# A hand-written scheduler with new transfer times: output projection two blocks late, q weights in halves, LayerNorm in pairs of tiles

## The chip, the cores and the metric

The kernel runs on one core of a Trainium2 chip. Time is device time in microseconds (us) for one execution. The core has a matrix engine (PE, TensorE; PEld is its weight load), a vector engine (DVE), an engine for activation functions (ACT), a general one (POOL, GpSimd) and one that issues transfers (SP). Each engine executes its own instructions in the order of the program, and they wait for each other through semaphores.

## The reference: what is computed

One layer of attention with 16 query heads that share one key and one value head, then a layer that sends 8 chosen tokens through a gated feed-forward network. x has 2048 tokens of 448 channels; a head has 28.

```
x = A_x
h = x + _A_ref(_layernorm(x))        # q = x wq (16 heads), k = x wk, v = x wv,
                                     # softmax(q k^T / sqrt(28)) v, then wo
h2 = h + _B_ref(_layernorm(h))       # r = x w_r; the 8 tokens with the largest r:
                                     # silu(x wg) * (x wu), then wd, times sigmoid(r);
                                     # the other tokens pass unchanged
```

## The kernel before

**Tiles and blocks.** The 2048 tokens are 16 tiles of 128. Attention runs over 16 blocks of queries (one tile each, all heads). A block has 64 score tiles of 128 keys by 512 query columns: 16 key tiles j times 4 groups of heads i, each in one row strip of PE.

**Two ways to the exponential.** ACT does most tiles: PE writes up to three score tiles into three PSUM banks (0 to 2 for even units, 3 to 5 for odd ones), and one ACT instruction (L712, `act_unit`) turns them into P. In blocks 1 to 15, 16 of the 64 tiles go through DVE instead: PE writes one score tile with each unit into bank 6 (VB), DVE rounds it to the bits of a bf16 exponential (Y, L737), and after four such tiles a batch is shifted into three further copies, two by DVE and one by POOL (Y, L746 and L748). The matmuls with V (`act_pv`, `dve_pv`) add P and the four Y copies into bank 7 (ACC). A block of 48 ACT tiles is so cut into 17 units, "slots" 0 to 16, of three tiles each but for three that have two. `TWO` names these three. A two-wide unit has a bank to spare, which can be lent: before, in slot 5 to the q projection of block b+2, in slot 10 to nothing (that slot carries no DVE tile either), in slot 14 to the output projection of block b-1. The borrowed bank has to be copied out by DVE before the unit but one may write it. P has room for 24 tiles and the P·V matmuls are due `LAG` = 4 units behind.

**Closing a block.** When all P·V matmuls of a block are done, DVE copies ACC to Ot (`close_acc`, L757), due 5.2 units into the next block. `post_block` (L592) then sends the softmax denominators through DRAM: Ot to scratch, back in another layout (Lc), a reciprocal on DVE (Rc, L596), to scratch, and back broadcast over partitions (Rb). POOL multiplies Ot by Rb into On, in two halves (L602). `out_proj` (L605) then multiplies On by wo on PE, adds x on DVE (hbuf, L610), takes LayerNorm 2 of the tile (statistics on DVE, a power and two scalings on POOL, L622, L637, L640) and the router's product (junk, r_col, L643 and L646).

**The head.** x, wk, wq and wv are loaded; ACT copies the weights into padded layouts (wk_rep, wq_pad); LayerNorm 1 (`ln1`, L524) runs by groups of tiles: one, one, two, and then four at a time. The first three groups take the root as Ln and Exp on ACT and are normalised on DVE (xn, L541); the others take a power on POOL and are normalised on POOL (L550) with a product nmr from DVE. `kv` (L554) transposes the normalised tiles on PE and makes K and V from them. Key tile j is needed by the units of block 0 in the order of j.

**The tail.** After the last block come the ranking of the router's values, the expert layer for the 8 tokens, and the output.

**Who sets the order.** All instructions are first collected as operations with an engine, a duration in ns, what they read and write, and a due time (`prio`, from `at(...)`, in tiles of ACT's work: a block is 64). `_Graph.plan` (L145) then plays the program through in Python: each engine takes the ready operation with the smallest due time; DVE holds itself back for the operations marked urgent (`dve_choice`); PE has rules of its own for changes of mode, and idle stretches in the plan are filled with multiplications by zero. The order found this way is fixed in the program. A result counts as available when its operation ends plus a latency of the engine; for a transfer that was 2000 ns after the issue, whatever its size and however many were under way. If a transfer takes longer on the chip than in the plan, an instruction that waits for it holds up all that the plan put behind it on its engine.

Of the kernel before, what the change touches and what calls it, by code (L numbers as in the profile page):

```python
# [19 lines left out]
class _Op:  # L20
    __slots__ = ("eng", "fns", "dur", "lat", "deps", "prio", "idx", "dma", "start", "end", "sig", "name",
                 "pred_left", "succs", "ready", "mode", "pos", "hold", "port", "urgent", "blk")


class _Graph:

    LAT = {PE: 217.0, AC: 185.0, DV: 140.0, PO: 190.0, SP: 0.0}
    SWITCH = 95.0
# [16 lines left out]
    def op(self, eng, fns, dur, reads=(), writes=(), prio=None, dma=False, name="", mode=None, pos=(0, 1, 2, 3),  # L45
           hold=None, deps=(), port=False, urgent=False, blk=None):
        o = _Op()
        o.eng, o.dur, o.dma, o.name = eng, float(dur), dma, name
        o.mode, o.pos, o.hold, o.port, o.urgent, o.blk = mode, pos, hold, port, urgent, blk
        o.fns = list(fns) if isinstance(fns, (list, tuple)) else [fns]  # L50
        o.lat = 2000.0 if dma else self.LAT[eng]
# [93 lines left out]
    def plan(self):  # L145
# [15 lines left out]
        self.todo = {}  # L161
# [9 lines left out]
        while left:  # L171
# [142 lines left out]
def _main(nc, G, sb, ps, psb, flag, scr, A_x, A_wq, A_wk, A_wv, A_wo, B_w_r, B_w_gate, B_w_up, B_w_down, out,  # L314
# [22 lines left out]
    nmr = sb("nmr", [128, NT], F32)  # L337
# [96 lines left out]
    def dma(o, i, writes, reads=(), prio=None):  # L434
        return G.op(SP, lambda e: e.dma_start(o, i), 60, reads=reads, writes=writes, dma=True, prio=prio)  # L435

    dma(x_sb[:, 0, :], x_v[:, 0, :], [("x", 0)])
    dma(wk_sb[0:CK, :, :], A_wk.rearrange("(k p) n -> p k n", p=CK), ["wk_sb"])
    dma(wq_sb[0:CK, :, :], A_wq.rearrange("(k p) n -> p k n", p=CK), ["wq_sb"])
    dma(x_sb[:, 1, :], x_v[:, 1, :], [("x", 1)])  # L440
    dma(x_sb[:, 2:4, :], x_v[:, 2:4, :], [("x", t) for t in range(2, 4)])
    dma(wv_sb[0:CK, :, :], A_wv.rearrange("(k p) n -> p k n", p=CK), ["wv_sb"])
    for i in range(4, NT, 4):
        dma(x_sb[:, i:i + 4, :], x_v[:, i:i + 4, :], [("x", t) for t in range(i, i + 4)])
# [29 lines left out]
    for h in range(2):  # L474
        G.op(AC, lambda e, h=h: e.activation(
            wq_pad[0:CK, 2 * h:2 * h + 2, :, :].rearrange("p k g (i c) -> p k (g i) c", c=32)[:, :, :, 0:DH],
            wq_sb[0:CK, 2 * h:2 * h + 2, :].rearrange("p k (h d) -> p k h d", d=DH), ACT.Identity), 950,
            reads=["wq_sb"], writes=["wq_pad"])
# [5 lines left out]
    for i in range(4):  # L484
        dma(wo_pad[32 * i + 1:32 * i + 1 + DH, :, :], wo_v[i], ["wo_pad"])
    dma(w_rb[:, :], B_w_r.partition_broadcast(128), ["w_rb"])
    dma(wg_sb[0:CK, :, :], B_w_gate.rearrange("(k p) n -> p k n", p=CK), ["wg_sb"])
    dma(wu_sb[0:CK, :, :], B_w_up.rearrange("(k p) n -> p k n", p=CK), ["wu_sb"])
    dma(wd_sb[:, :, :], B_w_down.rearrange("(k p) n -> p k n", p=128), ["wd_sb"])
# [32 lines left out]
    GROUPS = [[0], [1], [2, 3], [4, 5, 6, 7], [8, 9, 10, 11], [12, 13, 14, 15]]  # L522

    def ln1(c):  # L524
# [10 lines left out]
        if c < 3:  # L535
# [56 lines left out]
    def post_block(b):  # L592
# [6 lines left out]
        dma(Rb[:, rb, :], scr[b, 1].unsqueeze(1).broadcast_to([4, 32, 512]), [("Rb", rb)], reads=[("scr1", b)])  # L599
# [52 lines left out]
    TWO = (5, 10, 14)  # L652
    LAG = 4
    slots = []
# [11 lines left out]
    for x in vt:  # L666
        if slots[n][0] and slots[n][1] == TWO[1]:
            n += 1
        slots[n][3] = x
        n += 1  # L670
# [133 lines left out]
    else:  # L804
# [22 lines left out]
        for b in range(NB):  # L827
            at(64.0 * b + 64.0 + (LAG + 1.2) * m0, close_acc, b)
            if b:
                if b + 2 < NB:  # L830
                    at(64.0 * b + TWO[0] * m0 + 0.1, lambda b=b: q_project(b + 2, misc(b, TWO[0])))
                at(64.0 * b + TWO[2] * m0 + 0.1, out_proj, b - 1, misc(b, TWO[2]))
        for b in (1, 2):
            at(24.0 + 8 * b, lambda b=b: q_project(b, ring_bank()))
        at(64.0 * NB + (LAG + 1.3) * m0, out_proj, NB - 1, 0)
        for c in range(len(GROUPS)):
            t = 4.0 * GROUPS[c][0]
            at(t - (40.0 if c < 4 else 24.0), ln1, c)
            at(t - (39.9 if c < 4 else 23.9) , kv, c)
# [198 lines left out]
```

## Time and profile before

| | us |
|---|---|
| median of 3 runs | 496.29 |
| lowest and highest | 489.58, 497.11 |
| the profiled execution | 492.97 |
| its span, first to last instruction | 491.2 |
| PE, DVE, ACT, POOL busy in it | 347.6, 339.8, 372.7, 198.7 |
| first exponential of block 0, of block 1 | 15.20, 51.35 |
| last exponential ends | 431.77 |

How to read the rows: "L712" is a line of the kernel. A row of the timeline has the start, the length, the engine, the line, the operation, what it writes and reads, their shapes, how many instructions are merged, and in brackets the idle time of the engine ahead of it and what ended it. A row of waits has the total, the number and the longest. A row of the chain of waits has a start, a length and the name of what the end waited for. In a table of stretches each engine has its busy time and number of instructions, then come the granted clock of PE and the share and rate of the transfers. All matmuls are recorded under L418 and all transfers under L435, so they are told apart by what they write and read; "ps" is any PSUM bank.

### The profile page before, as it was taken

The page shows a single profiled execution, that of the slowest core. Times are in us where ns is not written, and L with a number is a line of the kernel's source. Part 1 is how long each engine was busy: PE and PEld are TensorE (multiplying, and loading weights), DVE is VectorE, ACT ScalarE, POOL GpSimd, SP SyncE. Part 2 cuts the span into 40 slices and gives each one's busy share as a digit, 9 for nine tenths or more (in the row PEclk, how much of TensorE's full clock was granted, in tenths as well). Part 3 has the DMA queues.
Part 4 walks back from the last instruction along what each step waited for, and adds up shares of the span by engine and source line. Part 5 has one row for each costly group of instructions (what it writes and reads, how often), then busy time and mean ns, then how long its engine had stood idle before and what let it go on. Part 6 is the DMA issues. An engine that isn't in the chain of part 4 may idle for free.

```text
span 491.2 us, 8685 instructions
## 1 busy us (share of the span) xinstructions
PE 347.6 (71%) x3571; PEld 118.9 (24%) x3571; DVE 339.8 (69%) x675; ACT 372.7 (76%) x305; POOL 198.7 (40%) x197
## 2 busy tenths in 40 slices
PE   1888777786768777876777776777786777711585
PEld 1443222122221222121212121212122222200540
DVE  6943778586967787687868586959586878634423
ACT  3579899888987989798979688978888899911012
POOL 3670344354544444344444453525444444641000
PEclk9799999889997999799989699989879999965565
DMA  8950000000000000000000000000000000000004
GB/s 226 247 144 7 3 24 3 22 3 24 3 23 1 24 1 25 1 25 1 25 2 21 3 3 23 3 21 3 23 1 24 3 24 3 24 22 3 0 3 155
DMA packets 15958, 14.69 MB, mean 30 GB/s; under 512 B 5976, under 2 KB 12904, under 8 KB 15912
## 3 DMA queue, kind: packets, MB, share of 16 engines
q1 hardware_dynamic: 15912, 14.05, 10.0%
q8 instruction: 31, 0.51, 0.4%
q14 instruction: 15, 0.12, 0.1%
HBM read 11.94 MB, written 2.10 MB: 29 GB/s over the span
## 4 chain that ended last, share of the span: by engine, by line
DVE 36%; PE 24%; DMA 19%; POOL 9%; ACT 6%; issue 3%; SPq 1%; POOLq 0%
PE ps L418 23%; DVE Y L737 16%; DMA Rb<-l_scr 14%; DVE Y L746 8%; ACT P L712 6%; POOL Y L748 5%; DMA l_scr<-Rc 4%; POOL On L602 3%; DVE Q L518 2%; DVE Ot L757 2%; DVE hbuf L610 2%; DVE junk L643 2%; DMA x_sb<-in_A_x_dram 1%; DVE r_col L646 1%; SPq L435 1%
## 5 line engine op out<-in xcount | busy, mean ns | idle before, releaser
L712 ACT ACTIVATE P<-ps 128x1536 bf16<-128x1536 f32 (+2 forms) x281 | 361.4, 1378 | 59.1 <-PE ps L418 57.7
L737 DVE TENSOR_SCALAR Y<-ps 128x512 int16<-128x512 f32 x240 | 164.9, 687 | 93.9 <-PE ps L418 93.1
L748 POOL TENSOR_TENSOR Y<-Y,step 128x1024 int32<-128x1024 int32 x60 | 113.5, 1892 | 147.7 <-DVE Y L746 110.7
L418 PE MATMUL ps<-Q,K 32*128 32x512 bf16 x1024 | 119.3, 401 | 75.7 <-DVE Y L737 49.6
L418 PE MATMUL ps<-Y,Vs 128*32 128x512 bf16 x960 | 93.2, 404 | 21.5 <-POOL Y L748 19.0
L746 DVE TENSOR_SCALAR Y<-Y 128x2048 int16<-128x2048 int16 x120 | 86.9, 735 | 0.1
L418 PE MATMUL ps<-P,Vs 128*32 128x512 bf16 x784 | 77.5, 401 | 0.6 <-ACT P L712 0.6
L418 PEld LDWEIGHTS ps<-Q,K 32*128 32x128 bf16 x1024 | 32.9, 91 | 180.9 <-ACT P L712 116.1
L602 POOL TENSOR_TENSOR On<-Ot,Rb 128x256 bf16<-128x256 f32 x32 | 24.3, 763 | 62.6 <-DMA Rb<-l_scr 62.6
L418 PE MATMUL ps<-zero 128*32 128x512 bf16 x107 | 38.3, 422 | 0.0
L418 PEld LDWEIGHTS ps<-Y,Vs 128*32 128x32 bf16 x960 | 23.6, 95 | 57.9 <-POOL Y L748 23.0
L418 PEld LDWEIGHTS ps<-P,Vs 128*32 128x32 bf16 x784 | 18.8, 94 | 39.6 <-issue 36.7
L418 PE MATMUL ps<-wo_pad,On 128*128 128x448 bf16 x64 | 19.2, 428 | 8.2 <-POOL On L602 8.2
L637 POOL TENSOR_SCALAR x_sb<-hbuf,st 128x448 bf16<-128x448 f32 x15 | 17.6, 1170 | 4.8 <-DVE st L626 4.8
L418 PE MATMUL ps<-xnT,wq_pad 112*128 112x128 bf16 x256 | 18.2, 226 | 0.1
L610 DVE TENSOR_TENSOR hbuf<-ps,x_sb 128x448 f32<-128x448 f32 x16 | 9.8, 616 | 10.0 <-PE ps L418 10.0
L418 PEld LDWEIGHTS ps<-xnT,wq_pad 112*128 112x128 bf16 x256 | 15.1, 101 | 4.0 <-issue 3.6
L940 ACT ACTIVATE xnT<-ps 128x448 bf16<-128x448 f32 x8 | 4.4, 545 | 12.9 <-PE ps L418 12.9
L421 PE MATMUL ps<-ident,xn 128*112 128x128 bf16 x64 | 6.0, 249 | 10.6 <-DVE xn L541 10.6
L418 PEld LDWEIGHTS ps<-zero 128*32 128x32 bf16 x107 | 9.2, 99 | 17.0 <-issue 15.0
L518 DVE TENSOR_SCALAR Q<-ps,qone 128x512 bf16<-128x512 f32 x16 | 11.8, 738 | 2.0 <-PE ps L418 2.0
L622 POOL TENSOR_TENSOR st<-st,nhalf 128x1 f32<-128x1 f32 x15 | 8.3, 552 | 11.0 <-DVE st L614 11.0
(125 smaller groups left out, 204.8 us busy)
## 6 DMA issues: line engine op xcount, KB each, us to landing
Rb<-l_scr SPq DMA_DIRECT2D x16, 256.0 KB
out_dram<-xnT SPq DMA_DIRECT2D x4, 448.0 KB, 3.3
wg_sb<-in_B_w_gate_dram SPq DMA_DIRECT2D x1, 1568.0 KB, 13.5
wu_sb<-in_B_w_up_dram SPq DMA_DIRECT2D x1, 1568.0 KB, 19.7
wd_sb<-in_B_w_down_dram SPq DMA_DIRECT2D x1, 1568.0 KB, 23.3
x_sb<-in_A_x_dram SPq DMA_DIRECT2D x3, 448.0 KB, 6.0
wq_sb<-in_A_wq_dram SPq DMA_DIRECT2D x1, 392.0 KB, 4.1
wo_pad<-in_A_wo_dram SPq DMA_DIRECT2D x4, 98.0 KB
```

What stands on the lines that cost most here:

```text
L418: return lambda e: e.matmul(o, lhsT=l, rhs=r, start=start, stop=stop)
L518: G.op(DV, lambda e: e.tensor_scalar(Q[:, q, :, :].rearrange("p g n -> p (g n)"), ps[:, bank, :], qone[:, 0:1], None, ALU.add), dvt(512), ...
L602: G.op(PO, lambda e, c=c: e.tensor_tensor(On[:, rb, c], Ot[:, rb, c], Rb[:, rb, c], ALU.mult), 750, reads=[("Ot", rb), ("Rb", rb)], writes ...
L610: G.op(DV, lambda e: e.tensor_tensor(hbuf[:, hr, :], ps[:, bank, 0:D], x_sb[:, t, :], ALU.add), dvt(D), reads=[pk(bank), ("x", t)], writes ...
L622: G.op(PO, lambda e: e.tensor_tensor(st[:, t, 4:5], st[:, t, 7:8], nhalf[:, 0:1], ALU.pow), 600, reads=[("st7", t), "nhalf"], writes=[("st ...
L637: G.op(PO, lambda e: e.tensor_scalar(outf[:, t, :], hbuf[:, hr, :], st[:, t, 5:6], st[:, t, 6:7], ALU.mult, ALU.add), 800, reads=[("h", hr ...
L643: G.op(DV, lambda e: e.scalar_tensor_tensor(junk[:, :], hbuf[:, hr, :], st[:, t, 4:5], w_rb[:, :], ALU.mult, ALU.mult, accum_out=st[:, t, ...
L712: G.op(AC, lambda e: e.activation(P[:, s0:s0 + w, :], ps[:, b0:b0 + w, :], ACT.Exp, bias=-(ZERO + SHIFT) * OCT, scale=OCT), w * 427 + 50, ...
L737: G.op(DV, lambda e: e.tensor_scalar(Y[:, y, 0, q, :].bitcast(I16), ps[:, VB, :], 0.0, 32639.0 - STEP[3], ALU.max, ALU.min), dvt(512), rea ...
L746: done = [G.op(DV, lambda e, c=c: e.tensor_single_scalar(y[c].bitcast(I16), y[0].bitcast(I16), STEP[c], ALU.add), 600, reads=r, writes=[(" ...
L748: G.op(PO, lambda e: e.tensor_tensor(y[3].bitcast(I32), y[0].bitcast(I32), step3[:, 0:1].broadcast_to([128, 1024]), ALU.add), 2050, reads= ...
L757: o = G.op(DV, lambda e: e.tensor_copy(Ot[:, b % 2, :], ps[:, ACC, :]), dvt(512), reads=[pk(ACC)], writes=[("Ot", b % 2)], prio=G.prio - 1 ...
```

## The change

The planner gets other times. A transfer is available 2700 ns after its issue instead of 2000, and Rb's 3900. Loads from the inputs carry their size (`kb`): their landing is counted from a running time at which the transfers before them are done, at 0.19 kB per ns. An operation of DVE or ACT that waits for one on the same engine gets its result after 85 or 110 ns instead of 140 or 185. Some of the work is moved or cut otherwise:

- wq is loaded in two halves, each needed by one of the two ACT copies into wq_pad; wv is loaded ahead of x tiles 2 and 3.
- LayerNorm 1 and `kv` run in groups of 1, 1, 2, 2, ... tiles. The first five groups (tiles 0 to 7) use Ln and Exp on ACT, the other four the power on POOL; all tiles are normalised on DVE. nmr and the POOL scaling are gone.
- The slots with two tiles are 2, 5 and 11. The output projection of block b-2 is due in slot 2 of block b, the q projection of b+2 in slot 5, and slot 11 carries no DVE tile. The projection of block 14 comes at the end of the stream in the DVE tiles' bank, that of block 15 after it as before.
- The q projections of blocks 1 and 2, made in block 0, are due at 14 and 34 instead of 32 and 40; groups up to tile 7 are due 40 ahead of their use, the others 24.

```diff
@@ _Graph
+    SELF = {DV: 85.0, AC: 110.0}
...
-        o.lat = 2000.0 if dma else self.LAT[eng]
+        o.lat = 2700.0 if dma else self.LAT[eng]
...
-        self.todo = {}
+        self.todo, self.dma_end = {}, 700.0
...
+                if c.dma and c.kb:
+                    self.dma_end = max(self.dma_end, s + 2100.0) + c.kb / 0.19
+                    c.lat = self.dma_end - c.end
...
-                r = c.end + c.lat if (sem or n.eng != c.eng) else c.start
+                r = c.end + (self.SELF.get(n.eng, c.lat) if n.eng == c.eng else c.lat) if (
+                    sem or n.eng != c.eng) else c.start
@@ _main: loads
-    dma(x_sb[:, 0, :], x_v[:, 0, :], [("x", 0)])
-    dma(wk_sb[0:CK, :, :], A_wk.rearrange("(k p) n -> p k n", p=CK), ["wk_sb"])
-    dma(wq_sb[0:CK, :, :], A_wq.rearrange("(k p) n -> p k n", p=CK), ["wq_sb"])
-    dma(x_sb[:, 1, :], x_v[:, 1, :], [("x", 1)])
-    dma(x_sb[:, 2:4, :], x_v[:, 2:4, :], [("x", t) for t in range(2, 4)])
-    dma(wv_sb[0:CK, :, :], A_wv.rearrange("(k p) n -> p k n", p=CK), ["wv_sb"])
+    load_x(0, 1)
+    dma(wk_sb[0:CK, :, :], A_wk.rearrange("(k p) n -> p k n", p=CK), ["wk_sb"], kb=25)
+    for h in range(2):
+        dma(wq_sb[0:CK, 2 * h:2 * h + 2, :], wq_v[:, 2 * h:2 * h + 2, :], [("wq_sb", h)], kb=196)
+    load_x(1, 2)
+    dma(wv_sb[0:CK, :, :], A_wv.rearrange("(k p) n -> p k n", p=CK), ["wv_sb"], kb=25)
+    load_x(2, 4)
...
-            reads=["wq_sb"], writes=["wq_pad"])
+            reads=[("wq_sb", h)], writes=["wq_pad"])
@@ _main: LayerNorm 1
-    GROUPS = [[0], [1], [2, 3], [4, 5, 6, 7], [8, 9, 10, 11], [12, 13, 14, 15]]
+    GROUPS = [[0], [1], [2, 3], [4, 5], [6, 7], [8, 9], [10, 11], [12, 13], [14, 15]]
...
-        if c < 3:
+        if c < 5:
...
-            G.op(DV, lambda e: e.scalar_tensor_tensor(nmr[:, sl], mv[:, sl, 0], -1.0, rstd[:, sl], ALU.mult, ALU.mult),
-                 80, reads=[("mv", t) for t in tl] + [("rstd", c)], writes=[("nmr", c)])
             for t in tl:
-                G.op(PO, lambda e, t=t: e.tensor_scalar(xn[:, t, :], x_sb[:, t, :], rstd[:, t:t + 1], nmr[:, t:t + 1],
-                                                        ALU.mult, ALU.add), 770,
-                     reads=[("x", t), ("nmr", c), ("rstd", c)], writes=[("xn", t)])
+                G.op(DV, lambda e, t=t: e.tensor_scalar(xn[:, t, :], x_sb[:, t, :], mv[:, t, 0:1], rstd[:, t:t + 1],
+                                                        ALU.subtract, ALU.mult), 300,
+                     reads=[("x", t), ("mv", t), ("rstd", c)], writes=[("xn", t)])
@@ post_block
-        dma(Rb[:, rb, :], scr[b, 1].unsqueeze(1).broadcast_to([4, 32, 512]), [("Rb", rb)], reads=[("scr1", b)])
+        dma(Rb[:, rb, :], scr[b, 1].unsqueeze(1).broadcast_to([4, 32, 512]), [("Rb", rb)], reads=[("scr1", b)]).lat = 3900.0
@@ the stream
-    TWO = (5, 10, 14)
+    TWO = (2, 5, 11)
...
-        if slots[n][0] and slots[n][1] == TWO[1]:
+        if slots[n][0] and slots[n][1] == TWO[2]:
             n += 1
...
-                    at(64.0 * b + TWO[0] * m0 + 0.1, lambda b=b: q_project(b + 2, misc(b, TWO[0])))
-                at(64.0 * b + TWO[2] * m0 + 0.1, out_proj, b - 1, misc(b, TWO[2]))
+                    at(64.0 * b + TWO[1] * m0 + 0.1, lambda b=b: q_project(b + 2, misc(b, TWO[1])))
+                if b > 1:
+                    at(64.0 * b + TWO[0] * m0 + 0.1, out_proj, b - 2, misc(b, TWO[0]))
         for b in (1, 2):
-            at(24.0 + 8 * b, lambda b=b: q_project(b, ring_bank()))
+            at(20.0 * b - 6.0, lambda b=b: q_project(b, ring_bank()))
+        at(64.0 * NB - 0.1, out_proj, NB - 2, VB)
...
-            at(t - (40.0 if c < 4 else 24.0), ln1, c)
-            at(t - (39.9 if c < 4 else 23.9) , kv, c)
+            at(t - (40.0 if c < 5 else 24.0), ln1, c)
+            at(t - (39.9 if c < 5 else 23.9), kv, c)
```

More of the change, by code (lines that the diff above doesn't have):

```diff
@@ L21 @@
     __slots__ = ("eng", "fns", "dur", "lat", "deps", "prio", "idx", "dma", "start", "end", "sig", "name",
-                 "pred_left", "succs", "ready", "mode", "pos", "hold", "port", "urgent", "blk")
+                 "pred_left", "succs", "ready", "mode", "pos", "hold", "port", "urgent", "blk", "kb")
 class _Graph:
     LAT = {PE: 217.0, AC: 185.0, DV: 140.0, PO: 190.0, SP: 0.0}
+    SELF = {DV: 85.0, AC: 110.0}
     SWITCH = 95.0
@@ L432, in _main, with dma, load_x @@
     x_v = A_x[0].rearrange("(n p) d -> p n d", p=128)
-    def dma(o, i, writes, reads=(), prio=None):
-        return G.op(SP, lambda e: e.dma_start(o, i), 60, reads=reads, writes=writes, dma=True, prio=prio)
-    dma(x_sb[:, 0, :], x_v[:, 0, :], [("x", 0)])
-    dma(wk_sb[0:CK, :, :], A_wk.rearrange("(k p) n -> p k n", p=CK), ["wk_sb"])
-    dma(wq_sb[0:CK, :, :], A_wq.rearrange("(k p) n -> p k n", p=CK), ["wq_sb"])
-    dma(x_sb[:, 1, :], x_v[:, 1, :], [("x", 1)])
-    dma(x_sb[:, 2:4, :], x_v[:, 2:4, :], [("x", t) for t in range(2, 4)])
-    dma(wv_sb[0:CK, :, :], A_wv.rearrange("(k p) n -> p k n", p=CK), ["wv_sb"])
+    def dma(o, i, writes, reads=(), prio=None, kb=0):
+        return G.op(SP, lambda e: e.dma_start(o, i), 60, reads=reads, writes=writes, dma=True, prio=prio, kb=kb)
+    def load_x(a, b):
+        dma(x_sb[:, a:b, :], x_v[:, a:b, :], [("x", t) for t in range(a, b)], kb=112 * (b - a))
+    wq_v = A_wq.rearrange("(k p) n -> p k n", p=CK)
+    load_x(0, 1)
[5 more added lines that the diff above has]
+    load_x(2, 4)
     for i in range(4, NT, 4):
-        dma(x_sb[:, i:i + 4, :], x_v[:, i:i + 4, :], [("x", t) for t in range(i, i + 4)])
+        load_x(i, i + 4)
     G.op(PO, lambda e: e.iota(idi[:, :], [[1, 128]], base=0, channel_multiplier=-1), 250, writes=["junk"])
```

15 lines of the change are left out of this document (7 added, 8 removed).

## The prediction

> **What bounds the kernel now.** I read the page first, then the waits, then the chain of waits, and last the timelines of ACT and POOL through one block of attention, because shares over the whole span mix a head, sixteen blocks and a tail.
>
> ```profile
> PE 347.6 (71%) x3571; PEld 118.9 (24%) x3571; DVE 339.8 (69%) x675; ACT 372.7 (76%) x305; POOL 198.7 (40%) x197
> POOL On L602 <- DMA Rb<-l_scr: 62.6, 16, 5.7
> ACT P L712 <- PE ps L418: 57.7, 64, 4.3
> ```
>
> No engine is full. ACT, which does the exponentials, is the fullest, and the time it loses is lost waiting for scores from PE (57.7 us in 64 waits). POOL loses 62.6 us in 16 waits, one a block, for the transfer that broadcasts the softmax denominators (Rb). POOL is only 40% busy, so the question is what stands behind it in its queue.
>
> ```profile
> 189.75 4.64 DMA Rb<-l_scr
> ...
> 208.96 0.60 DVE Ot L757
> ...
> 213.27 0.66 DVE Q L518
> ...
> 216.13 4.85 DMA Rb<-l_scr
> 221.04 0.73 POOL On L602
> 221.77 1.86 POOL Y L748
> 223.68 2.30 PE ps L418 x19
> 226.00 0.69 DVE Y L737
> 226.70 0.54 DVE hbuf L610
> ...
> 235.11 0.60 DVE junk L643 x2
> ...
> 241.02 4.63 DMA Rb<-l_scr
> ```
>
> This is the chain through one block, each line starting where the one above released it. Rb lands 4.85 us after its issue. Only then does POOL multiply (On); only after that does it make the fourth copy of a batch of shifted scores (Y L748), which the P·V matmuls on PE wait for; and the next score matmuls stand behind those in PE's order. The batch had nothing to do with Rb. From Rb to Rb this block took 241.02 - 216.13 = 24.89 us and the one ahead of it 216.13 - 189.75 = 26.38 us.
>
> ```profile
> 86.64 4.98 DMA Rb<-l_scr
> ...
> 397.62 4.62 DMA Rb<-l_scr
> ```
>
> Twelve such periods, blocks 2 to 13, take (397.62 - 86.64) / 12 = 25.92 us each.
>
> ```profile
> 214.51 9.08 ACT L712 ACTIVATE P<-ps 128x1536 bf16<-128x1536 f32 x7 [0.90 <-PE ps L418]
> 224.45 1.02 ACT L712 ACTIVATE P<-ps 128x1024 bf16<-128x1024 f32 x1 [0.85 <-PE ps L418]
> 226.00 1.45 ACT L712 ACTIVATE P<-ps 128x1536 bf16<-128x1536 f32 x1 [0.53 <-PE ps L418]
> 228.00 2.79 ACT L712 ACTIVATE P<-ps 128x1536 bf16<-128x1536 f32 x2 [0.55 <-PE ps L418]
> ```
>
> ACT's own view of that block has four holes. The first, 0.90, comes from the q projection: its bank is copied late, as the chain shows (Q at 213.27, behind a DVE queue). The second, 0.85, is the batch held up by Rb. The third and fourth, 0.53 and 0.55, are the output projection and its copy (hbuf, 226.70). So ACT without holes needs 24.89 - 2.83 = 22.0 us a block; the seven units from 214.51 give 9.08 / 20 = 0.454 us a tile, and 48 tiles make 21.8, which agrees.
>
> **The change, part by part.** *Measured transfer times in the planner.* No instruction is added. The planner believed a transfer lands 2.0 us after issue; with the new 2.7 and, for Rb, 3.9, its sum from the accumulator copy (Ot) to On rises from about 8.7 to 12.7 us (0.14 + three times 2.76 or 2.06, 3.96 or 2.06, and the reciprocal).
>
> ```profile
> 227.90 1.89 POOL L748 TENSOR_TENSOR Y<-Y,step 128x1024 int32<-128x1024 int32 x1 [3.60 <-DVE Y L746]
> ```
>
> On the chip Ot ends at 209.56 and Rb lets On start at 221.04, 11.5 us later. So On will be planned behind the batch of 221.77 and in front of that of 227.90, seen here in POOL's timeline, where Rb has landed and a POOL hole of 3.60 us takes both halves (2 x 0.73). Queued behind On are then only that later batch and the LayerNorm steps of an output projection; none waits for a transfer. The 0.85 goes to zero.
>
> *Output projection two blocks late.* Moved are four matmuls, hbuf, two statistics steps, one power on POOL, two small DVE steps, two POOL scalings, the router product and its sum; no transfer is among them. It passes POOL's next two batches and the whole q projection on PE and DVE, and gets some 4 us between On and its use where it had none (13.8 slots of 1.3 us, less 12.7 and the two halves). Its own price remains: four matmuls, then a bank that DVE must copy before the next unit but one may write it. The nearest rows are in the last block, where On was in time:
>
> ```profile
> 405.79 1.45 ACT L712 ACTIVATE P<-ps 128x1536 bf16<-128x1536 f32 x1 [0.26 <-PE ps L418]
> 407.79 10.67 ACT L712 ACTIVATE P<-ps 128x1536 bf16<-128x1536 f32 x8 [0.55 <-PE ps L418]
> ```
>
> That is 0.26 + 0.55 = 0.81, against 0.53 + 0.55 = 1.08 now; below, 0.5 would remain if hbuf met an empty DVE. I take 0.81. *The q projection* keeps slot 5; whether DVE is free for its copy depends on an order that I can't see, so 0.3 to 0.90, and I take 0.90. Two-wide slots are still three a block, at other places: nothing. A block then takes 22.0 + 0.90 + 0.81 = 23.7 us (22.8 to 24.0), a gain of 2.2 us, and twelve of them 26.6. Blocks 1, 14 and 15 lack one of the two projections and hardly change. The last projection but one now falls after the stream; its steps hide under the last block's own Rb chain, 11.5 us long, in which POOL otherwise idles: nothing, or the 0.81 of one projection if that cover failed.
>
> *The head.* These are rows of DVE and ACT, in the order of time:
>
> ```profile
> 2.88 0.63 DVE L529 BATCH_NORM_STATS2 bn<-x_sb 128x6 f32<-128x448 bf16 x1 [0.28 <-DMA x_sb<-in_A_x_dram]
> ...
> 6.01 0.63 DVE L529 BATCH_NORM_STATS2 bn<-x_sb 128x6 f32<-128x448 bf16 x1 [2.44 <-DMA x_sb<-in_A_x_dram]
> 10.08 0.69 DVE L541 TENSOR_SCALAR xn<-x_sb,mv,rstd 128x448 bf16<-128x448 bf16 x2
> ```
> ```profile
> 5.74 1.93 ACT L475 ACTIVATE wq_pad<-wq_sb 112x896 bf16<-112x896 bf16 x2 [1.82 <-DMA wq_sb<-in_A_wq_dram]
> ...
> 15.20 3.71 ACT L712 ACTIVATE P<-ps 128x1536 bf16<-128x1536 f32 x3 [3.89 <-PE ps L418]
> 20.20 3.28 ACT L712 ACTIVATE P<-ps 128x1024 bf16<-128x1024 f32 x3 [1.29 <-PE ps L418]
> 27.82 6.89 ACT L712 ACTIVATE P<-ps 128x1536 bf16<-128x1536 f32 x6 [4.33 <-PE ps L418]
> ...
> 51.35 1.45 ACT L712 ACTIVATE P<-ps 128x1536 bf16<-128x1536 f32 x1 [0.61 <-PE ps L418]
> ```
>
> Tile 0 has its statistics at 3.51, and then DVE stands 2.44 us in front of tile 1, which the old plan thought there; the normalised tile comes at 10.08. With tile 1 planned behind it, xn can follow at about 5. The next to be late is wq_pad, finished at 7.67 now; in halves, ACT can start on the first about 1 us sooner, so about 6.7. The extra issue on SP delays the later x tiles by half a microsecond, which nothing near them waits for. The first exponentials start at about 10.7 instead of 15.20. From there block 0 can be bound by ACT or by DVE, which loses 0.16 of nmr for each group of four and gains the xn of twelve tiles from POOL.
>
> ```profile
> L529 DVE BATCH_NORM_STATS2 bn<-x_sb 128x6 f32<-128x448 bf16 x16 | 9.5, 607 | 3.5 <-DMA x_sb<-in_A_x_dram 3.5
> L565 DVE COPY xnT<-ps 112x1024 bf16<-112x1024 bf16 x7 | 4.7, 687 | 4.3 <-PE ps L421 4.3
> L531 DVE BATCH_NORM_AGGREGATE mv<-bn 128x2 f32<-128x6 f32 x16 | 2.3, 163 | 0.0
> ...
> L541 DVE TENSOR_SCALAR xn<-x_sb,mv,rstd 128x448 bf16<-128x448 bf16 x4 | 1.4, 384 | 0.0
> ...
> L575 DVE TENSOR_SCALAR K<-ps,kb 128x256 bf16<-128x256 f32 x1 | 0.5, 468 | 0.0
> ...
> L582 DVE TENSOR_TENSOR Vs<-ps,vone 128x64 bf16<-128x64 f32 x1 | 0.2, 215 | 0.0
> L533 DVE TENSOR_SCALAR var<-mv 128x2 f32<-128x2 f32 x1 | 0.2, 160 | 0.0
> ```
>
> A pair costs DVE 2 x (0.607 + 0.163 + 0.384) + 0.687 + 0.468 + 2 x 0.215 + 0.160 = 4.05 us (Vf is priced as Vs); seven pairs from about 8.5, when tile 0's steps are done, end at 37 with the two Q copies still to come. ACT needs 10.7 + 64 x 0.454 = 39.8, and has the Ln and Exp of two more groups. So ACT bounds it by a little, and I allow 2.7 us for those and for holes where there were 1.29 + 4.33: block 1 starts at 42.5 instead of 51.35, a gain of 8.8 (11 with no holes, 4.5 if only the start moves).
>
> *Sum.* 491.2 - 26.6 - 8.8 = 455.8, and 492.97 - 491.2 = 1.8 around the span makes 457.6. The profiled execution lies 0.7% under the median of the runs; I predict 457 for the median.
>
> **A rule against it.** The granted clock:
>
> ```profile
> 193.00:198.00 5.00, 2.71 (x33) 0.81 (x26) 2.08 (x4) 4.36 (x5) 3.26 (x3) 1.00 0.04 14
> 198.00:203.00 5.00, 4.55 (x32) 0.82 (x30) 3.32 (x6) 2.68 (x3) 0.87 (x1) 0.52 0.00 0
> ```
>
> PE was busy 2.71 of 5 us around the hold-up behind Rb, and the granted clock (the column after POOL) then falls to 0.52. That is why blocks of 26.38 and 24.89 alternate, and my 23.7 takes the full clock. The Trainium skill, in TensorE: Matmul & The Clock Gate, section What's actually happening, gives the loss only to a window of about 3.4 us without work. By that rule gaps of this size neither cost the clock nor give it back, and the loss would stay; the rows, with work in every such stretch, speak against it.
>
> **The rivals.** *The clock still falls in every second block.* It costs (26.38 - 24.89) / 2 = 0.75 a block, 9 in all: 466. For it speaks that PE still pauses at both projections, against it that the longest pause is the one removed. *DVE is crowded.* hbuf, statistics, Ot, Q and the router product now fall together in slots 2 to 7. With Ot's 0.60 and Q's 0.66 on the chain, and 0.6 for each of the others, that is 3.0 us; the Y tiles (0.69) leave 0.67 in each unit of 1.36 us (three tiles at 0.454), 4.0 in six slots, of which four batch copies take 2.4. The 1.4 too much would meet a bank that PE waits for: 1.4 x 13 = 18, 475. Against it: statistics and product may slip. *Only the head moves, and little:* the stream takes another wait as long as the one removed, and block 0 is bound by DVE: 492.97 - 4.5 = 488.5. *Slower:* Ot is planned behind the whole chain of the output projection, eight slots long now. P has room for 24 tiles, eight units, and P·V runs about five behind, so from 3.7 us of lateness ACT stops; a chain of 8.4 us (hbuf at 226.70 to junk at 235.11) costs 4.7 a block, 13 x 4.7 = 61: 518. Against it: the planner gives Ot the higher rank.
>
> **How the numbers follow.** Forecast 0.58, clock 0.12, crowded DVE 0.16, head only 0.09, slower 0.05. The forecast's own bounds are 457 - 2.2 - 12 x 0.9 = 444 and 457 + 4.3 + 12 x 0.3 = 465; up to 476 the range takes in the clock and the crowded DVE. Three runs of before lie 1.5% apart, so some 2% can be told from no change: faster 0.86 (the first three), same 0.09, slower 0.05.
>
> **What would show it.** Right: On waits for Rb no longer, or under 5 us before the last block; a period of Rb near 23.7; first exponentials near 10.7 and block 1 near 42.5; granted clock at 1.0 through the stream; ACT holes only at the two projections. Wrong: a POOL hole ended by Rb; Ot later against its block; DVE without holes while ACT has them; a hole of 2 us at Q or hbuf.

## The result and the profile after

| | before | after |
|---|---|---|
| median of 4 runs, us | 492.94 | 457.36 |
| lowest and highest | 488.21, 497.11 | 456.32, 458.43 |
| the profiled execution, its span | 492.97, 491.2 | 457.83, 455.6 |
| first exponential of block 0, of block 1 | 15.20, 51.35 | 11.32, 50.96 |
| last exponential ends | 431.77 | 396.96 |

The ratio of the times is 0.9313 (0.9239 to 0.9387). Ratios here and below leave out runs that had a lower granted clock than the others of their kernel; the profiled run of one experiment, x3, is of that kind. The forecast of 457 was met, but the last two rows of the table already say that it was not met in the way it was made: block 1 starts 0.4 us sooner, not 8.8, and the stretch from there to the last exponential shrank from 380.4 to 346.0 us, by 34.4 and not by 26.6.

The page of after, with the busy times, the granted clock in 40 slices, and the engines' shares of the chain that ended last:

```profile
PE 335.5 (74%) x3583; PEld 121.5 (27%) x3583; DVE 343.5 (75%) x696; ACT 370.3 (81%) x309; POOL 188.6 (41%) x198
PEclk9999999999999999999999999999999999955565
DVE 49%; PE 32%; ACT 10%; issue 5%; POOL 1%; DMA 1%; POOLq 0%; SPq 0%
```

The waits of after (total, number, longest):

```profile
ACT P L719 <- PE ps L422: 26.7, 31, 3.0
POOL On L609 <- DMA Rb<-l_scr: 7.3, 2, 5.3
```

The old wait of 62.6 us in 16 is 7.3 in 2, and one of the two is the last block's own. ACT's wait for scores has halved. The clock's row shows 9 from the first slice to the end of the stream, where before it dipped every third slice or so. Two pieces at half speed hide in it: the head, shown below, and 55.70 to 59.11, where the column reads 0.50. POOL's timeline in one block shows the order that the forecast described:

```profile
207.88 1.41 POOL L609 TENSOR_TENSOR On<-Ot,Rb 128x256 bf16<-128x256 f32 x2
211.77 1.90 POOL L755 TENSOR_TENSOR Y<-Y,step 128x1024 int32<-128x1024 int32 x1 [2.48 <-DVE Y L753]
```

The multiplication On has no idle time in front of it, and the batch behind it waits for its own data. ACT's timeline of this block and the next has one hole a block:

```profile
198.98 18.24 ACT L719 ACTIVATE P<-ps 128x1536 bf16<-128x1536 f32 x14
218.19 7.96 ACT L719 ACTIVATE P<-ps 128x1536 bf16<-128x1536 f32 x6 [0.96 <-PE ps L422]
```

Four holes (0.90, 0.85, 0.53, 0.55) have become one of 0.96. What makes it stands in PE's timeline and then DVE's:

```profile
214.14 0.93 PE L422 MATMUL ps<-wo_pad,On 128*128 128x448 bf16 x4
...
217.74 0.40 PE L422 MATMUL ps<-Q,K 32*128 32x512 bf16 x4 [0.22 <-DVE hbuf L617]
...
219.26 0.40 PE L422 MATMUL ps<-xnT,wq_pad 112*128 112x128 bf16 x4
```
```profile
216.38 0.68 DVE L764 COPY Ot<-ps 128x512 f32<-128x512 f32 x1
216.98 0.61 DVE L617 TENSOR_TENSOR hbuf<-ps,x_sb 128x448 f32<-128x448 f32 x1
...
219.99 0.74 DVE L527 TENSOR_SCALAR Q<-ps,qone 128x512 bf16<-128x512 f32 x1
```

The projection is done at 215.07, but DVE copies Ot first and hbuf, which frees the bank, second, so the score matmuls start only at 217.74. The q projection, done at 219.66, has its copy at 219.99 and costs ACT nothing. Block 0 went otherwise. ACT's timeline:

```profile
11.32 1.45 ACT L719 ACTIVATE P<-ps 128x1536 bf16<-128x1536 f32 x1 [3.02 <-PE ps L422]
...
18.64 3.28 ACT L719 ACTIVATE P<-ps 128x1024 bf16<-128x1024 f32 x3 [1.20 <-PE ps L422]
24.26 2.37 ACT L719 ACTIVATE P<-ps 128x1536 bf16<-128x1536 f32 x2 [2.33 <-PE ps L422]
...
45.66 2.37 ACT L719 ACTIVATE P<-ps 128x1536 bf16<-128x1536 f32 x2 [1.55 <-PE ps L422]
...
50.96 3.71 ACT L719 ACTIVATE P<-ps 128x1536 bf16<-128x1536 f32 x3 [0.61 <-PE ps L422]
```

and PE's, with the stretches 18 to 24 and 24 to 28 us (length, then busy times of PE, PEld, DVE, ACT, POOL):

```profile
7.70 1.86 PE L422 MATMUL ps<-xnT,wq_pad 112*128 112x128 bf16 x16 [0.61 <-DVE mv L540]
...
24.55 1.10 PE L425 MATMUL ps<-ident,xn 128*112 128x128 bf16 x8
...
29.11 0.65 PE L425 MATMUL ps<-ident,xn 128*112 128x128 bf16 x8
```
```profile
18.00:24.00 6.00, 5.54 (x38) 2.43 (x38) 4.85 (x18) 3.28 (x3) 1.97 (x6) 1.00 1.03 218
24.00:28.00 4.00, 4.00 (x27) 1.80 (x23) 2.68 (x8) 3.16 (x3) 1.50 (x5) 1.00 1.07 251
```

The same eight transposes take 1.10 us at 24.55 and 0.65 at 29.11: until about 28.4 PE runs at half speed, and from 18 to 28 it is busy nearly all the time (9.54 of 10 us) while ACT waits. The clock's column says 1.00 here only because this trace has no clock record before that point; the lengths of the matmuls tell.

### The profile page after: what moved, and what is told of

Read it like the earlier page. It is cut to its first block, busy times and chain, and to the rows that moved or that the text cites. A ratio compares the mean times of both kernels' runs of the same rounds, so it can differ in the third digit from the quotient of the medians.

```text
span 455.6 us, 8732 instructions
## 1 busy us (share of the span) xinstructions
PE 335.5 (74%) x3583; PEld 121.5 (27%) x3583; DVE 343.5 (75%) x696; ACT 370.3 (81%) x309; POOL 188.6 (41%) x198
## 4 chain that ended last, share of the span: by engine, by line
DVE 49%; PE 32%; ACT 10%; issue 5%; POOL 1%; DMA 1%; POOLq 0%; SPq 0%
PE ps L422 30%; DVE Y L744 24%; ACT P L719 10%; DVE Y L753 8%; DVE bn L619 2%; DVE junk L650 2%; DVE Q L527 2%; DVE Ot L764 2%; DVE hbuf L617 2%; DVE r_col L653 2%; PE ps L425 1%; DVE xnT L572 1%; DVE K L582 1%; DMA wq_sb<-in_A_wq_dram 1%; DVE idx L886 1%
## 5 line engine op out<-in xcount | busy, mean ns | idle before, releaser
L719 ACT ACTIVATE P<-ps 128x1536 bf16<-128x1536 f32 (+2 forms) x281 | 358.3, 1401 | 29.1 <-PE ps L422 26.7
L744 DVE TENSOR_SCALAR Y<-ps 128x512 int16<-128x512 f32 x240 | 165.3, 689 | 58.6 <-PE ps L422 58.5
L422 PE MATMUL ps<-Q,K 32*128 32x512 bf16 x1024 | 112.9, 388 | 61.1 <-DVE Y L744 45.6
L422 PE MATMUL ps<-Y,Vs 128*32 128x512 bf16 x960 | 88.2, 388 | 17.7 <-DVE Ot L764 11.3
L753 DVE TENSOR_SCALAR Y<-Y 128x2048 int16<-128x2048 int16 x120 | 82.6, 688 | 0.1
L422 PE MATMUL ps<-P,Vs 128*32 128x512 bf16 x784 | 75.7, 389 | 0.5 <-ACT P L719 0.5
L422 PE MATMUL ps<-zero 128*32 128x512 bf16 x107 | 32.8, 386 | 0.0
L644 POOL TENSOR_SCALAR x_sb<-hbuf,st 128x448 bf16<-128x448 f32 x15 | 14.8, 984 | 31.4 <-DVE st L633 31.4
L422 PE MATMUL ps<-xnT,wq_pad 112*128 112x128 bf16 x256 | 20.6, 229 | 0.6 <-DVE mv L540 0.6
L422 PE MATMUL ps<-wo_pad,On 128*128 128x448 bf16 x64 | 15.8, 369 | 6.5 <-POOL On L609 6.5
L595 POOL TENSOR_SCALAR Vs<-Vf 128x64 bf16<-128x64 f32 (+1 forms) x36 | 9.0, 249 | 22.7 <-DVE Vf L592 21.0
L422 PEld LDWEIGHTS ps<-zero 128*32 128x32 bf16 x107 | 10.2, 97 | 7.0 <-issue 1.0
```

The costliest lines, as they stand in the source:

```text
L422: return lambda e: e.matmul(o, lhsT=l, rhs=r, start=start, stop=stop)
L644: G.op(PO, lambda e: e.tensor_scalar(outf[:, t, :], hbuf[:, hr, :], st[:, t, 5:6], st[:, t, 6:7], ALU.mult, ALU.add), 800, reads=[("h", hr ...
L719: G.op(AC, lambda e: e.activation(P[:, s0:s0 + w, :], ps[:, b0:b0 + w, :], ACT.Exp, bias=-(ZERO + SHIFT) * OCT, scale=OCT), w * 427 + 50, ...
L744: G.op(DV, lambda e: e.tensor_scalar(Y[:, y, 0, q, :].bitcast(I16), ps[:, VB, :], 0.0, 32639.0 - STEP[3], ALU.max, ALU.min), dvt(512), rea ...
L753: done = [G.op(DV, lambda e, c=c: e.tensor_single_scalar(y[c].bitcast(I16), y[0].bitcast(I16), STEP[c], ALU.add), 600, reads=r, writes=[(" ...
```

## The experiments

Eleven kernels; what was expected of each was written before it ran. The table has the median time, the ratio to before on the same chip, the first exponentials of blocks 0 and 1, and the stream, which is the time from block 1's first exponential to the end of the last. These last three columns are from the profiled execution.

| kernel | us | ratio (95%) | block 0 | block 1 | stream |
|---|---|---|---|---|---|
| before | 492.94 | 1 | 15.20 | 51.35 | 380.4 |
| after | 457.36 | 0.931 (0.924, 0.939) | 11.32 | 50.96 | 346.0 |
| x1_times | 485.54 | 0.971 (0.956, 0.986) | 15.83 | 53.06 | 371.2 |
| x2_late | 456.45 | 0.918 (0.909, 0.927) | 15.98 | 52.25 | 341.8 |
| x3_head | 499.12 | none | 11.24 | 53.84 | 383.4 |
| x4_warm | 451.49 | 0.907 (0.899, 0.915) | 10.89 | 45.34 | 344.8 |
| c_after | 458.51 | 0.926 (0.918, 0.933) | 11.11 | 50.75 | 346.0 |
| x5_hbuf | 451.21 | 0.907 (0.899, 0.915) | 11.10 | 53.58 | 335.3 |
| x6_nofill | 485.45 | 0.978 (0.969, 0.988) | 11.25 | 54.05 | 369.0 |
| x7_both | 441.74 | 0.889 (0.881, 0.896) | 10.38 | 44.83 | 335.8 |
| x8_fours | 452.15 | 0.918 (0.910, 0.926) | 10.76 | 46.37 | 344.9 |
| x9_warmbefore | 494.41 | none | 16.41 | 52.19 | 382.3 |
| x10_latewarm | 454.76 | 0.922 (0.915, 0.929) | 15.60 | 49.79 | 341.7 |

Before gave 498.85, 496.91 and 497.94 beside x1 to x4, c to x7 and x8 to x10. x3's ratio, 0.978 (0.969 to 0.986), rests on two of its ten runs, 484.03 and 489.48, and is left out of the table; x9's runs (489.77 to 503.01) lie within before's beside them (484.58 to 504.95), and no ratio is formed.

**The measured transfer times alone** (x1), in before: the four transfers of `post_block` get 2700, 2700, 2700 and 3900 ns.

```diff
-        dma(scr[b, 0], Ot[0:128:32, rb, :], ..., reads=[("Ot", rb)])
+        dma(scr[b, 0], Ot[0:128:32, rb, :], ..., reads=[("Ot", rb)]).lat = 2700.0
...
-        dma(Rb[:, rb, :], ..., reads=[("scr1", b)])
+        dma(Rb[:, rb, :], ..., reads=[("scr1", b)]).lat = 3900.0
```

> The kernel before with one thing of the change: the planner's latency of post_block's four transfers (2700, 2700, 2700, 3900 ns); slots, projection one block late and head stay. If the hold-up of POOL behind Rb is the cost, On goes behind the batch that it held up, the granted clock stays at 1.0, and the period from Rb to Rb falls from 25.9 to about 24.3: 473 us in all. If the projection needs its second block of delay, PE now waits for On at the projection in the place of the batch: period about 25.5, 488 us.

**The late output projection alone** (x2), in before: the two-wide slots, the block that `out_proj` belongs to and the extra call at the end, with the old 2000 ns.

```diff
-    TWO = (5, 10, 14)
+    TWO = (2, 5, 11)
...
-                at(64.0 * b + TWO[2] * m0 + 0.1, out_proj, b - 1, misc(b, TWO[2]))
+                if b > 1:
+                    at(64.0 * b + TWO[0] * m0 + 0.1, out_proj, b - 2, misc(b, TWO[0]))
...
+        at(64.0 * NB - 0.1, out_proj, NB - 2, VB)
```

> The kernel before with the slots (2, 5, 11) and the output projection two blocks late, and the old latency of 2000 ns everywhere. If the hold-up behind Rb is a matter of the planned time alone, POOL still waits for Rb ahead of a batch, some 4 us in every block, and the period stays at 25 or more: 480 to 493 us. If the later projection is what frees the block, the period falls to about 23.5: 463 us.

With the times alone the stream takes 371.2 us: On goes behind the batch that it held up, and its wait for Rb is about 1 us in most blocks. The projection, still one block late in slot 14, is then the largest hole. x1's waits and ACT's timeline:

```profile
POOL On L602 <- DMA Rb<-l_scr: 16.8, 13, 5.7
```
```profile
201.82 10.67 ACT L712 ACTIVATE P<-ps 128x1536 bf16<-128x1536 f32 x8 [1.35 <-PE ps L418]
213.38 11.45 ACT L712 ACTIVATE P<-ps 128x1536 bf16<-128x1536 f32 x9 [0.88 <-PE ps L418]
226.18 10.66 ACT L712 ACTIVATE P<-ps 128x1536 bf16<-128x1536 f32 x8 [1.35 <-PE ps L418]
```

Two holes are left, 1.35 at the projection (PE waits 0.81 for hbuf at 201.19) and 0.88 at the q projection, 24.36 us from one 1.35 to the next. With the late projection alone, the stream takes 341.8 us, less than with the whole change. x2's waits and ACT's timeline, then rows of DVE and PE at its second hole:

```profile
ACT P L712 <- PE ps L418: 21.1, 23, 4.5
POOL On L602 <- DMA Rb<-l_scr: 17.2, 9, 5.2
```
```profile
195.42 26.02 ACT L712 ACTIVATE P<-ps 128x1536 bf16<-128x1536 f32 x20 [0.96 <-PE ps L418]
221.93 18.20 ACT L712 ACTIVATE P<-ps 128x1536 bf16<-128x1536 f32 x14 [0.49 <-PE ps L418]
```
```profile
220.59 0.74 DVE L518 TENSOR_SCALAR Q<-ps,qone 128x512 bf16<-128x512 f32 x1
...
221.48 0.40 PE L418 MATMUL ps<-Q,K 32*128 32x512 bf16 x4 [0.24 <-ACT P L712]
```

These two holes take turns from block to block. In every second block DVE copies Ot ahead of hbuf and the hole is 0.96, as in after; in the others hbuf (215.48) goes ahead of Ot (216.76), and 0.49 are left behind the q projection: the scores of the next unit start at 221.48, 0.15 us after the copy Q ends at 221.33. The profile names ACT as the releaser there, but before and x1 have the same 0.15 us between the end of Q and the scores behind it (213.92 and 214.07, 212.78 and 212.94).

POOL still waits for Rb 17.2 us in 9 blocks here, because the planner still believes in 2.0 us, and ACT does not notice: what stands behind On is now LayerNorm 2 of a projection, not a batch. So the measured times are not needed. Moving the projection is enough to take the batch out from behind the wait, and with it in place the rest of the change brings the stream nothing (346.0 against 341.8). Nor does it bring the whole kernel anything that shows: x2's ratio is 0.918 (0.909 to 0.927), that of the whole change 0.931 beside its own before and 0.926 (0.918 to 0.933) in c. x2 moves the two-wide slots and delays the projection by a block in one step; which of the two does it was not tried.

**The head alone** (x3), in before: the loads with their sizes, wq in halves, pairs, all tiles normalised on DVE, and the due times of the head.

> The kernel before with the head of the change alone: loads with sizes, wq in halves, LayerNorm 1 and kv in pairs, all normalised on DVE, q projections of blocks 1 and 2 due earlier; stream and other latencies as before. The prediction's 8.8 us of gain would give 484 us with block 1 starting at 42.5. If the changed kernel's trace holds here too, the first exponential is at 11.3 but block 1 starts at about 51 as before: 492 us, no difference.

The exponentials start at 11.24 instead of 15.20, and block 1 does not start sooner (53.84 against 51.35). The transposes and projections run at half speed until about 37 us. Its median equals before's (499.12 and 498.85), and its ten runs reach from 484.03 to 501.69, so that the worth of the head by itself stays undecided here; what the profile shows is an earlier start that block 0 spends again, as in after.

**The matmuls by zero from the start of the program** (x4), in after. The planner fills PE's idle time with them in the stream only; here it may do so from the moment that their operand is set, and the head has four banks instead of five.

```diff
+    def early(self, s, c):
+        t = max(max(self.pe_free), self.zero.end + 190.0)
+        if not self.zero.end or t + 216.0 + self.SWITCH > s + 1.0 or self.recent(s) >= self.FLOOR:
+            return None
+        o = self.filler(0)
...
+        if b is None and not self.after and min(self.pe_free) >= 0.0:
+            return self.early(s, c)
...
-    head_banks = [R0, R1, 4, 3, ACC]
+    head_banks = [R0, R1, 4, 3]
```

> The changed kernel with more multiplications by zero: the planner's own rule for filling idle PE time now holds from the start of the program and not only from the first P.V matmul on (some 20 more zero matmuls in the first 15 us; one PSUM bank fewer for the first two tiles). Clock theory: in the changed kernel PE runs at half clock until 28.4 us, which stretches the chain of block 0; here the clock is full by about 10 us, block 1 starts at about 45 instead of 51, and the time is about 452 us. Rival, two banks: the pairs use three of two free PSUM banks in turn and wait for each other, the clock aside; block 1 still starts at 50 to 51 and the time stays at 457 us.

PE's timeline of x4, then ACT's, then two of its stretches:

```profile
2.42 4.45 PE L433 MATMUL ps<-zero 128*32 128x512 bf16 x10 [2.42 <-POOL zero L479]
...
8.28 1.07 PE L433 MATMUL ps<-xnT,wq_pad 112*128 112x128 bf16 x16
```
```profile
10.89 1.45 ACT L731 ACTIVATE P<-ps 128x1536 bf16<-128x1536 f32 x1 [2.21 <-PE ps L433]
...
17.16 3.28 ACT L731 ACTIVATE P<-ps 128x1024 bf16<-128x1024 f32 x3 [0.56 <-PE ps L433]
21.42 20.99 ACT L731 ACTIVATE P<-ps 128x1536 bf16<-128x1536 f32 x18 [0.98 <-PE ps L433]
...
45.34 3.71 ACT L731 ACTIVATE P<-ps 128x1536 bf16<-128x1536 f32 x3 [0.61 <-PE ps L433]
```
```profile
12.00:18.00 6.00, 5.07 (x51) 2.57 (x52) 6.00 (x24) 4.54 (x10) 1.86 (x8) 1.00 1.01 255
18.00:24.00 6.00, 4.63 (x59) 2.54 (x57) 6.00 (x22) 5.02 (x6) 2.58 (x7) 1.00 1.04 242
```

The same 16 matmuls of the q projection take 1.07 us instead of 1.86. (The four transposes ahead of them still took 0.68, where four at full speed take 0.43 at 10.94: the full clock came at about 8.1.) The holes of 1.20 and 2.33 shrink to 0.56 and 0.98, and block 1 starts 5.6 us sooner than in after. The clock was what block 0 lost its gain to; that fewer banks would cost it did not show. At full clock the next bound is DVE, with no idle time from 12 to 24 us.

**After once more** (c), on the chip of the next three, to be compared with them.

> The changed kernel itself, on this chip, beside the others: 457 us, block 1 starting at 51, Rb period 23.0.

It repeats after: 458.51 us, block 1 at 50.75, the same stream.

**hbuf ahead of Ot** (x5), in after:

```diff
-             reads=[pk(bank), ("x", t)], writes=[("h", hr)], prio=G.prio - 900)
+             reads=[pk(bank), ("x", t)], writes=[("h", hr)], prio=G.prio - 1400)
```

> The changed kernel with one rank changed in the planner: the copy of the output projection out of its borrowed bank (hbuf) goes ahead of the copy of the accumulators (Ot) on DVE. If the only hole of ACT left in a block, 0.96 us, is PE waiting for hbuf behind Ot, the hole goes: period 22.2, 13 x 0.8 less, 446 us. Rival: Ot, 0.6 us later, holds up the P.V matmuls of the next block by as much, and the time stays at 457 us.

ACT's timeline of x5 in the same part of the stream:

```profile
215.12 21.96 ACT L719 ACTIVATE P<-ps 128x1536 bf16<-128x1536 f32 x17 [0.28 <-PE ps L422]
237.36 12.98 ACT L719 ACTIVATE P<-ps 128x1536 bf16<-128x1536 f32 x10 [0.28 <-PE ps L422]
```

The hole is 0.28, the period 237.36 - 215.12 = 22.24 instead of 23.03, and the stream 10.7 us shorter. So the one hole left was the order of two copies on DVE. The time fell by 7.3 us only. Block 1 started 2.8 later, as in this order of the head the half clock lasted until about 37 us. And the tail of this profile is 61.5 us where c's is 58.9; the cause of that was not looked for.

**No matmuls by zero at all** (x6), in after:

```diff
-    FLOOR = 0.5
+    FLOOR = 0.0
```

> The changed kernel without any of the 107 multiplications by zero that the planner puts into idle PE time. By the page's rule, a window without any work is needed to lose the clock; no pause of PE in the stream is near 3.4 us, so the clock stays at 1.0 and the time stays at 457 us or falls a little. By the rows of the kernel before, partly idle stretches are enough: the granted clock falls to 0.5 again and again in the stream, and the time rises by 0.75 us a block or more, to 467 us or above.

The page of x6, a row of PE's timeline, and stretches around it:

```profile
PEclk9999678999799959995789696599997895985566
```
```profile
214.78 0.40 PE L422 MATMUL ps<-Q,K 32*128 32x512 bf16 x4 [0.87 <-DVE Y L744]
```
```profile
205.00:210.00 5.00, 4.13 (x56) 1.32 (x55) 4.17 (x10) 4.88 (x5) 2.28 (x2) 1.00 0.05 7
210.00:215.00 5.00, 3.66 (x46) 1.09 (x42) 4.40 (x10) 5.00 (x5) 2.18 (x3) 1.00 0.15 51
215.00:220.00 5.00, 4.10 (x36) 0.87 (x36) 2.93 (x5) 4.88 (x5) 2.96 (x4) 0.58 0.00 2
```

The clock falls again and again, and the stream is 23.0 us longer than c's although 107 matmuls (32.8 us of PE's time) were left out. Here it fell after a stretch in which PE was busy 3.66 of 5 us and paused for 0.87 at most. So short pauses alone do not keep the full clock in after's stream; the filling is needed too.

**Early zeros and hbuf ahead of Ot together** (x7), in after, with the two edits of x4 and x5.

> The changed kernel with both: zero matmuls from the start on, and hbuf ahead of Ot. If the two causes are apart, the gains add: 457 - 5.9 - 11 = 440 us, block 1 starting at 45 and a period of 22.2.

441.74 us, 0.8887 (0.881 to 0.8964) of before: this beats both kernels. x7's waits, against 26.7 us in 31 in after:

```profile
ACT P L731 <- PE ps L433: 11.9, 25, 2.3
```

Block 1 starts at 44.83, the period is 22.23, and the two gains add: 50.75 - 44.83 = 5.9 at the head and 346.0 - 335.8 = 10.2 in the stream make 16.1. Against that stands a tail of 61.1 us instead of 58.9, so that the two profiled executions differ by 14.0 (457.95 and 443.91); the medians differ by 16.8.

**The late projection and early zeros, with the old head** (x10): x2's and x4's edits, in before.

> The kernel before with the output projection two blocks late in slots 2, 5 and 11 (as in the run that did that part alone) and with the zero matmuls let in from the start of the program (and one bank fewer in the head), but with the head of the kernel before: one q weight load, groups of four, old transfer times. It asks whether the head part is worth anything once the clock is full from the start. Theory (the head's new order does start the exponentials some 4 us sooner, and only PE at half clock ate that): first exponentials at 14 to 15 us instead of 10.89 and block 1 at 48 to 50 us instead of the 45.34 of the run that warms PE with the whole change, and a time of 453 to 456 us. Rival (the head part is worth nothing whatever the clock: DVE's or PE's own queue sets the end of block 0): block 1 at 45 to 46 us and a time of 450 to 452 us. In both the period of the blocks stays near 22.9 us.

**Early zeros in before** (x9): x4's edit alone.

> The kernel before with nothing but the zero matmuls let in from the start of the program (and one bank fewer in the head). Theory (PE at half clock is what lengthens block 0, in the kernel before in a stretch from 17.3 to 24.1 us): block 1 starts 1 to 3 us sooner than the 51.35 us of before, at 48 to 50, the stream keeps its period of some 25.9 us and its pieces of half clock, and the time is 491 to 495 us where before gives 493 to 497. Rival (a full clock from the start keeps the gate open through the stream as well, so that it is the start that costs the later pieces): no half clock at all later and a period of 24.9 us, 12 us less: 480 to 484 us.

**Early zeros, and fours instead of pairs** (x8): x4 with

```diff
-    GROUPS = [[0], [1], [2, 3], [4, 5], [6, 7], [8, 9], [10, 11], [12, 13], [14, 15]]
+    GROUPS = [[0], [1], [2, 3], [4, 5, 6, 7], [8, 9, 10, 11], [12, 13, 14, 15]]
...
-        if c < 5:
+        if c < 3:
...
```

> The kernel after with the zero matmuls let in from the start (as in the run that warms PE) and with the groups of the head put back from pairs to fours behind the first three, all still on DVE. It asks what the pairs are worth at full clock. Theory (pairs bring the first tiles of keys sooner, as the holes in ACT's row behind the first exponentials are waits for keys): ACT's holes in block 0 grow and block 1 starts at 46.5 to 49 us instead of 45.34; time 453 to 456 us. Rival (pairs only add work to DVE, 0.16 us and a bank each): block 1 at 43.5 to 45.3 us, time 449 to 451 us.

ACT's timelines of x10 and of x8, and PE's of x9 and of x10:

```profile
15.60 1.45 ACT L724 ACTIVATE P<-ps 128x1536 bf16<-128x1536 f32 x1 [3.96 <-PE ps L429]
...
49.79 3.71 ACT L724 ACTIVATE P<-ps 128x1536 bf16<-128x1536 f32 x3 [0.61 <-PE ps L429]
```
```profile
23.31 22.45 ACT L731 ACTIVATE P<-ps 128x1536 bf16<-128x1536 f32 x20 [3.07 <-PE ps L433]
46.37 3.71 ACT L731 ACTIVATE P<-ps 128x1536 bf16<-128x1536 f32 x3 [0.61 <-PE ps L433]
```
```profile
11.19 0.68 PE L432 MATMUL ps<-ident,xn 128*112 128x128 bf16 x4 [3.60 <-DVE xn L553]
...
12.76 1.89 PE L429 MATMUL ps<-xnT,wq_pad 112*128 112x128 bf16 x16
```
```profile
10.84 0.43 PE L432 MATMUL ps<-ident,xn 128*112 128x128 bf16 x4 [2.82 <-DVE xn L553]
...
12.17 1.89 PE L429 MATMUL ps<-xnT,wq_pad 112*128 112x128 bf16 x16
```

x10: block 0 takes 34.19 us from its first exponential, x4 34.45; what separates them is the start, 15.60 against 10.89. So the head's new order is worth 4.5 us (49.79 - 45.34) once the clock no longer takes it away. In the spans 1.7 of that are left (450.9 and 449.2), because x10's stream is 3.1 shorter, again the one planned with the old times; the medians, from different chips, are 3.3 apart. x8: pairs are worth 1.03 us (46.37 - 45.34; its theory gave 46.5 as the earliest start): a hole of 3.07 in place of 0.98, partly made up later. x9 answered neither of its theories. Its zeros end at 7.59, PE then has nothing to do for 3.60 us, and the q projection behind that is at half speed again (16 matmuls in 1.89 us from 12.76); block 1 starts at 52.19. x10 has such a pause too, of 2.82 us: the four transposes behind it still run at full speed (0.43), and then the q projection takes the same 1.89. So its clock was not full throughout either, which I estimate at 1.89 - 1.07, about 0.8 of its 4.5.

## Why the prediction was right in its total and wrong in two of its terms

**On behind the batch, the 0.85 goes to zero: right, but the cause given is the lesser one.** The forecast gave the merit to the measured times, and x1 shows that they do bring On behind the batch. They alone bring 380.4 - 371.2 = 9.2 us of stream, and x2 shows the late projection alone bringing 38.6, the wait for Rb left as it was planned before.

**A block of 23.7 us: it is 23.03.** The base of 22.0 was right: 23.03 - 0.96 = 22.07. "I take 0.90" for the q projection was the mis-sized term: its hole is gone, below the lower bound of 0.3. x1, with the old slots and the new times, still has 0.88 there in nearly every block; x2, with the new slots and the old times, has 0.49 in every second block and none in the others. So most of it went with the move; what took the rest was not tried. The projection's 0.81 became 0.96, since hbuf did not meet an empty DVE but stood behind Ot; x5, with the order turned, has 0.28, under the 0.5 that was given as the least. The terms 0.90 - 0.15 - 0.07 = 0.68 a block make 8.2 us in twelve blocks; the stream gained 34.4 - 26.6 = 7.8 more than forecast.

**"So ACT bounds it by a little": this step failed.** The first exponentials came at 11.32, where 10.7 was forecast, and then block 0 took 39.64 us instead of 42.5 - 10.7 = 31.8. The sum weighed ACT against DVE and left PE out, although before's own rows show it at half speed in block 0 (eight transposes take 1.10 us at 20.49 and 0.65 at 16.32). PE at half speed was the bound; x4 takes that away and gets 34.45. Of the 2.65 us still missing, 0.56 and 0.98 are holes of ACT in the first half of the block, with DVE full from 12 to 24 us: the seven pairs were costed by their sum, which ends in time, and not by when each key tile is due. The 8.4 us missing at the head and the 7.8 us too many in the stream cancel, by luck; with 0.8 from the tail, where nothing was forecast, that is why the total of 457 was met. A last step was lucky too: the sum gave 457.6 for a profiled execution, and the 0.7% by which that of before lay under its median would have made 461 of it; in after the profiled execution lies 0.1% above the median.

**The clock.** But for 3.4 us in block 1 it is 1.0 through the stream, as the forecast needs. The reason given, that the longest pause is removed, is half of it. Before has as many matmuls by zero as after (107) and loses the clock around the hold-up; x6 has no hold-up and loses it without them. The Trainium skill, in TensorE: Matmul & The Clock Gate, section What's actually happening, puts the loss down to a window of about 3.4 us without work. The traces disagree: no window without any work was needed. In x6 the clock fell at 215.83, and PE was busy for 1.98 of the 3.41 us ahead of that; in before it fell at 198.20, behind 1.84 of 3.41. In x9 it fell at 10.28, 2.7 us into the pause of 3.60, and in x10 at 11.15, when the pause of 2.82 was already over. The same section of the Trainium skill lets the full clock come after one busy window of that length. In after it came at 28.39, and the changes in that trace (28.39, 55.70, 59.11) lie 8 and 1 times 3.41 apart. A window on the same grid, 18.15 to 21.56, has PE recorded busy for 3.41 of 3.41 us, so that by that rule I estimate the full clock for 21.6; it did not come there, as the transposes at 24.55 show.

**The rivals.** *Crowded DVE* was right as a place, in the 0.96 and in block 0, and too dear: 1.4 us a block were feared, and the turned order of two copies in x5 takes away 0.96 - 0.28 = 0.68. *The clock still falls* came true where it was not looked for, in the head. *Slower, Ot behind the projection's chain*: Ot goes ahead of hbuf, which is what costs the 0.68. The last projection but one behind the stream cost nothing that shows: the tail is 58.6 us, before 59.4.

**What stays open.** Which work counts for the clock isn't settled: in x7 ten matmuls by zero over 3.82 us were enough, in x4 it took these, four transposes and two more by zero, and 9.54 of 10 us of the head's mixed work were not enough in after. The shorter latencies on the same engine were in no run by themselves. Why the half clock of the head lasted until 28.4 in after and c, and until 37 to 38 in x3, x5 and x6, whose heads are nearly the same, wasn't tried.

## What to carry to other kernels

When a slow transfer blocks a queue, moving its consumer to where nothing urgent stands behind it can be worth far more than a truer time in the planner: here the move alone gave the whole gain, with a wait of 17 us left standing. A sum for a stage has to name every engine in it with its rate at that moment, and the lengths of like matmuls early and late show a half clock where the record of the clock is missing. A total that is met proves none of its terms: add up the stages one by one.

## What the runs showed of the hardware that was not expected

- The matmuls by zero, 32.8 us of PE's time, are worth 369.0 - 346.0 = 23.0 us of this kernel's stream. Without them the clock falls behind pauses of under 0.9 us.
- Cut into windows of 3.41 us on the grid of its changes, the clock follows PE's share of busy time. Between the first record of the clock and the end of the exponentials, the thirteen profiles have 44 windows of full clock with a fall at their end, and PE was recorded busy for 60% or less in 40 of them (18 to 69% in all). Of the 1332 windows that kept the full clock, 20 had 60% or less and none less than 53%. It came back 44 times, always behind a window with about 90% or more; the head of after, where no such window was enough until 28.4, is not among these and stays unexplained.
- Half speed at the start of the program lasted 22 us from the first matmul (6.44 to about 28.4 in after). With matmuls of 512 columns by zero from 2.42 on the clock was full by 8.28 in x4: 5.6 to 5.9 us in block 1's start (50.96 to 45.34 from after to x4, 50.75 to 44.83 from c to x7).
- Rb took 4.6 to 5.1 us from its issue before; the plan with 2.0 and the plan with 3.9 were both short, and only the place of its consumer made it harmless.
